# A fused linear attention and Fourier layer on one core: the channel transform on rows folded a second time, with parts of the weight and table conversion on POOL and a longer fixed order

## The chip, the core and the metric

The kernel runs on one core of a Trainium2 chip. The core has a matrix engine (PE, with its weight loads shown apart as PEld), two engines for elementwise work that also read the accumulators in PSUM (DVE and ACT), a third that works on SBUF alone (POOL), and SP, which issues most DMAs. PSUM has eight banks here, each 128 partitions by 512 fp32 values. The metric is the time of one execution on the device in microseconds; before the change its median is 1025.26 us over three runs.

## What is computed

Linear attention with an RMS norm, then a layer that adds the real part of a two-dimensional Fourier transform, then a normalised two-matrix network:

```python
def _attn_ref(q, k, v, g_norm):
    kv = np.einsum('bhsd,bhse->bhde', k, v)
    out = np.einsum('bhsd,bhde->bhse', q, kv)
    rms = np.sqrt(np.mean(out * out, axis=-1, keepdims=True) + 1e-06)
    return (out / rms * g_norm).astype(np.float32)

def _moe_ref(x, w_ch1, w_ch2):
    X = np.fft.fft(x, axis=1)
    X = np.fft.fft(X, axis=2)
    u = x + np.real(X).astype(np.float32)
    mu = np.mean(u, axis=-1, keepdims=True)
    var = np.mean((u - mu) ** 2, axis=-1, keepdims=True)
    un = (u - mu) / np.sqrt(var + 1e-06)
    ch = np.maximum(un @ w_ch1, 0.0) @ w_ch2
    return (u + ch).astype(np.float32)
```

There are 8 batches of 8 heads, 576 positions and head size 64; x is the attention's output with the heads side by side, 8 x 576 x 512. The network goes from 512 to 2048 and back. The two weight matrices arrive as 64-bit floats and are converted on the chip. A product in fp32 accuracy is made of three passes of the type fp32r: high by high, high by low, low by high part.

## The kernel before

The work has two parts. The first (to about 320 us) does attention and transforms for the eight batches, and with free time on PE the first piece of the network. The second is the rest of the network, and runs in the order in which it is written.

**The transforms.** The sequence axis is folded: a tile `x` of 96 or 97 rows holds position p and its mirror 576 - p side by side (512 columns each), three tiles a batch (`t` = 0, 1, 2). `plan_fold` scales the rows, adds to each channel d the mirror channel 512 - d (the tile `ab`, columns d = 1 to 256), and then takes sum and difference of the two sides (`xe`), which are split into high and low parts (`xh`, `xl`). Part 0 is the cosine part, part 1 the sine part. `plan_seq` transforms along the sequence: for each part and each half of the 256 channels (`ch`) nine matmuls of 290 columns into one bank (L816), then the high part by ACT (L830) and the low part by DVE (L834) into `pt`. `plan_chn` transforms along the channels: per tile and part six matmuls (two halves by three passes) of 258 columns (L851) with the table `cd`. ACT copies the cosine part (`me`, L863), DVE adds and subtracts the sine part (`pm`, L871), and the results are added to `x` on both sides (L883, L886; on POOL but for batch 0). Then `x` goes to memory (`u_scr`), is transposed by PE (L942) and split again (`unT`, L951 and L954). Channel 0 adds the same to every channel; it is summed apart (`zero`, L779), transformed once for all batches (L1131) and added as a bias at the end.

**Weights.** There are 16 blocks of each matrix. `plan_w` converts one: ACT takes the upper word's magnitude (L352), five DVE steps follow (a clamp, L359, then L360 to L369), a sum (L986), for the first matrix a mean taken off with PE's help (L383, L389), and a split into high and low parts. Blocks 0 to 2 are converted during the first batches, blocks 3 to 6 at the end of the first part, the rest in the second part by `sum_w` and `split_w`.

**Early network.** For each of nine blocks of 512 rows `plan_early` computes, with weight blocks 0 to 2, three times 12 matmuls of 512 columns (L424) and four times 9 (L442).

**Order.** The first part is a list of operations with engine, planned cost in ns, rank, predecessors and ring buffers. `Plan.run` simulates it: each engine takes the ready operation of the lowest rank whose buffers are free. Ranks come from batch and stage (`rank`), with shifts from the table `SHIFT`; FFN work has ranks from 1000, and 45 spare operations (two matmuls of 512 columns each on a constant, L494) have the last rank of all and keep PE running in gaps. Up to plan time `PIN_UNTIL` (in ns, 95000) the instructions of all engines are bound to this order; later ones may be moved by the scheduler of the language. `W_CONV` and `W_RANK` are the ranks at which weight blocks 0 to 2 are converted and loaded. Operations marked `port` are not planned beside one on POOL. PSUM banks are a ring of eight (`p8`).

Of the kernel before, what the change touches and what calls it, by code (L numbers as in the profile page):

```python
# [9 lines left out]
F32 = mybir.dt.float32  # L10
# [31 lines left out]
W_CONV = (-60, 5, 6)  # L42
W_RANK = (-60, 4, 11)
# [6 lines left out]
PIN_UNTIL = 95000  # L50
# [8 lines left out]
    ("", "POOL", 20): 18,  # L59
    ("chn", "ACT", -34): 54.5,  # L60
    ("dft", "DVE", -35): 83.5,
    ("fold", "DVE", -36): -33.5,
    ("out", "DVE", -58): 31,
    ("out", "ACT", 2): 157,
    ("q", "PE", -39): 3,
    ("q", "PE", 21): -30,
    ("q", "ACT", 31): -19.5,
    ("q_load", "DMA", -39): -1.5,
# [5 lines left out]
    "x": 8, "raw": 2, "e2": 4, "wk": 2, "xhl": 3, "pt": 1, "two": 2,   # L74
# [178 lines left out]
def kernel(  # L253
# [14 lines left out]
    nc = tc.nc  # L268
# [9 lines left out]
    ND = DH + 2  # L278
    W = DH + 1
# [71 lines left out]
    def w_clear(raw, ps):  # L351
        nc.scalar.activation(ps, w_raw(raw).bitcast(F32)[:, :, 1], AF.Abs)  # L352

    def w_steps(raw, ps, pf):
# [4 lines left out]
            lambda: nc.vector.tensor_scalar(ps, ps, F64_TINY, F64_HUGE, ALU.max, ALU.min),  # L359
            lambda: nc.vector.tensor_scalar(  # L360
                a, a, 3, 0x3FFFFFFF, ALU.logical_shift_left, ALU.bitwise_and
# [99 lines left out]
    cd = cst.tile([P, 2, 2, 2, ND], F32R, name="cd")  # L461
# [41 lines left out]
    def plan_dft(part, dst, src, n, r, key):  # L503
        size = src.shape[-2] * src.shape[-1]
# [5 lines left out]
        for lo_, hi_ in ((0, n - n % 16), (n - n % 16, n)):  # L510
# [8 lines left out]
            "DVE", 200 + 1.6 * size if key == "s" else 200 + size, r,  # L519
            lambda: nc.vector.tensor_tensor(lo, raw.t[:n, :size], hi.bitcast(F32), ALU.subtract),  # L520
            [b], [raw],
        )
        dft[key, part] = c

    last_qkv = []

    def plan_kv(b):
# [7 lines left out]
        for pr in range(NPAIR):  # L535
# [46 lines left out]
            mm.append(op("PE", 1080, rank(b, KV), go, ld + lds, [ps, kvt] + ts + rest))  # L582
# [48 lines left out]
    def plan_q(b, side, j, qt, ld):  # L631
# [17 lines left out]
        tr = op("PE", 330, rank(b, QT), turn, ld, [qt, ps, fq])  # L649
# [102 lines left out]
    def plan_fold(b, t, x, y_done, yp, gs):  # L752
# [25 lines left out]
        def zero():  # L778
            nc.scalar.activation(  # L779
                x0[:n, t, b : b + 1], xv(0)[:, 0:1], AF.Identity, bias=xv(1)[:, 0:1]  # L780
            )

        def fold():
            xx = x.t[:n].rearrange("p (s d) -> p s d", s=2)
            nc.vector.tensor_tensor(  # L785
                two_of(ab), xx[:, :, 1 : DH + 1], xx[:, ::-1, DM - 1 : DH - 1 : -1], ALU.add
            )
# [7 lines left out]
        f = op("DVE", 690, r, fold, ms, [x, ab, xe], port=True)  # L795
        z = op("ACT", 300, r, zero, ms + [i_x0], [x])
# [10 lines left out]
    def plan_seq(b, grp, xs, pt, dones):  # L807
        part, ch = divmod(grp, 2)
        ps = bank_buf("ps_f")

        def mm():
            idx = 0
            for t in range(3):
                n = rows[t]
                for a, c in passes:
                    nc.tensor.matmul(  # L816
                        ps.t[:, :NS],
                        xs[t].t[a][:n, part, ch * P : (ch + 1) * P],
                        cs[:n, part, c, t, :],
                        start=(idx == 0),  # L820
                        stop=(idx == 8),
                    )
                    idx += 1

        r = rank(b, SEQ)
        a = op("PE", 1200, r, mm, dones + [dft["s", part]], [ps, pt] + xs)
        a.dense = True
        h = op(
            "ACT", 414, r - D2,
            lambda: nc.scalar.activation(pt.t[0][:, part, ch, :], ps.t[:, :NS], AF.Copy), [a], [ps, pt],  # L830
        )

        def low():
            nc.vector.tensor_tensor(  # L834
                pt.t[1][:, part, ch, :], ps.t[:, :NS], pt.t[0][:, part, ch, :].bitcast(F32), ALU.subtract
            )

        return op("DVE", 450, r - D2, low, [h], [ps, pt])

    def plan_chn(b, t, x, pt, dones):  # L840
# [3 lines left out]
        for part in range(2):  # L844
            ps = bank_buf("ps_f")

            def mm(part=part, ps=ps):
                idx = 0
                for ch in range(2):
                    for a, c in passes:  # L850
                        nc.tensor.matmul(  # L851
                            ps.t[:n, :ND],
                            pt.t[a][:, part, ch, offs[t] : offs[t] + n],
                            cd[:, part, c, ch, :],
                            start=(idx == 0),
                            stop=(idx == 5),
                        )
                        idx += 1

            pss.append(ps)  # L860
            mms.append(op("PE", 720, r, mm, dones + [dft["d", part]], [ps, pt]))
        me, pm = e2_buf("me"), e2_buf("pm")
        c = op("ACT", 400, r - D2, lambda: nc.scalar.copy(me.t[:n, :W], pss[0].t[:n, :W]), mms[:1], [pss[0], me, pm])  # L863

        def pmv():
            return pm.t[:n, : 2 * W].rearrange("p (s w) -> p s w", s=2)

        pms = []
        for s in range(2):
            def mix(s=s):  # L870
                nc.vector.scalar_tensor_tensor(  # L871
                    pmv()[:, s], pss[1].t[:n, :W], sgn_t[:n, s, 0:1], me.t[:n, :W], ALU.mult, ALU.add
                )
# [43 lines left out]
    def plan_turn(b, side, t, x, done):  # L917
# [27 lines left out]
        a = op("PE", 330, r, turn, done, [x, ps] + blocks)  # L945
# [491 lines left out]
```

## Time and profile before

| | us |
|---|---|
| median of 3 runs | 1025.26 (1024.71 to 1025.57) |
| profiled execution | 1022.79 |
| its span | 1021.0 |
| PE busy, with overlaps of pipelined matmuls | 1002.3 |
| first matmul starts | 10.36 |
| last matmul of the channel transform starts (L851) | 318.8 |

The span is what the trace covers; the profiled execution's own time has 1.8 us around it. Lines L... are those of the kernel before. In the views below PE stands for matmuls, PEld for weight loads; a group's row gives its count, busy time and mean duration, then the idle time of the engine ahead of it. A matmul's duration covers its way through the array, so matmuls in a row overlap; how much time a group of them takes is read from the chain of work, whose pieces have a start and a length.

### The profile page before, as it was taken

What the parts mean: (1) busy time and instruction counts of PE and PEld (TensorE: products, weight loads), DVE (VectorE), ACT (ScalarE), POOL (GpSimd) and SP (SyncE); (2) the same over time, 40 slices, a digit from 0 to 9 for tenths busy, and PEclk for the clock granted to TensorE, in tenths of its full rate; (3) what the DMA queues carried; (4) which work ended last, traced back from release to release, by engine and by line L of the source; (5) the groups of instructions that cost most, each with busy time, mean ns of one, the idle gap of its engine ahead of it and who ended that gap; (6) DMA issues with size and microseconds to landing.
All of it is one profiled execution on the core that took longest, in us unless ns stands there. A gap on an engine that the chain in (4) does not pass through costs nothing.

```text
span 1021.0 us, 15425 instructions
## 1 busy us (share of the span) xinstructions
PE 1002.3 (98%) x6070; PEld 844.0 (83%) x6070; DVE 475.3 (47%) x847; ACT 324.8 (32%) x657; POOL 314.4 (31%) x328
## 2 busy tenths in 40 slices
PE   5999999999999999999999999999999999999997
PEld 5898888889888888888888888888888888888886
DVE  4897656654788879997131313131221311311211
ACT  2666556554644434344221202121121120210110
POOL 0526768775675132235722303020020010100000
PEclk9999999999999999999999999999999999999999
DMA  9989778664346775645553514230320400400101
GB/s 250 212 230 282 181 209 258 162 170 131 137 163 213 268 253 191 236 129 170 161 179 86 180 59 150 82 125 0 141 67 1 165 21 1 165 0 1 42 1 42
DMA packets 109260, 140.74 MB, mean 138 GB/s; under 512 B 51854, under 2 KB 76482, under 8 KB 104580
## 3 DMA queue, kind: packets, MB, share of 16 engines
q1 hardware_dynamic: 105652, 132.28, 41.9%
q0 software_dynamic: 1920, 6.29, 1.9%
q10 hardware_dynamic: 1616, 1.18, 0.5%
q8 instruction: 48, 0.79, 0.3%
q14 instruction: 24, 0.20, 0.1%
HBM read 88.33 MB, written 51.40 MB: 137 GB/s over the span
## 4 chain that ended last, share of the span: by engine, by line
PE 97%; DMA 1%; ACT 0%; POOL 0%; DVE 0%; issue 0%; SPq 0%; DVEq 0%; POOLq 0%
PE ps_h L424 38%; PE acc L442 38%; PE ps_o L669 4%; PE ps_f L816 4%; PE ps_f L851 4%; PE ps_k L574 3%; PE ps_s L494 2%; PE ps_q L643 2%; PE ps_t L942 2%; DMA qt<-in_q_dram 1%; PE ps_w L383 1%; DMA vm<-in_v_dram 0%; POOL x L883 0%; ACT x L686 0%; DVE uu L1324 0%
## 5 line engine op out<-in xcount | busy, mean ns | idle before, releaser
L424 PE MATMUL ps_h<-unTh,w 128*128 128x512 f32 x1152 | 356.6, 391 | 1.2 <-ACT fq L647 1.2
L442 PE MATMUL acc<-w,hh 128*128 128x512 f32 x1152 | 345.5, 390 | 0.0
L437 DVE SCALAR_TENSOR_TENSOR hl<-ps_h,hh 128x512 fp32r<-128x512 f32 x144 | 99.1, 688 | 371.8 <-ACT hh L434 367.5
L442 PEld LDWEIGHTS acc<-w,hh 128*128 128x128 f32 x1152 | 215.1, 188 | 44.3
L424 PEld LDWEIGHTS ps_h<-unTh,w 128*128 128x128 f32 x1152 | 214.8, 188 | 44.8 <-ACT fq L647 1.4
L434 ACT ACTIVATE hh<-ps_h 128x512 fp32r<-128x512 f32 x144 | 85.8, 596 | 454.0 <-PE ps_h L424 439.2
L424 PE MATMUL ps_h<-unTl,w 128*128 128x512 f32 x576 | 224.3, 389 | 0.0
L442 PE MATMUL acc<-w,hl 128*128 128x512 f32 x576 | 213.5, 389 | 0.0
L424 PEld LDWEIGHTS ps_h<-unTl,w 128*128 128x128 f32 x576 | 108.1, 188 | 22.6
L442 PEld LDWEIGHTS acc<-w,hl 128*128 128x128 f32 x576 | 108.1, 188 | 22.6
L1271 POOL DMA_INDIRECT uu<-u_scr,rowidx x24 | 23.2, 968 | 285.1 <-DVE uu L1324 177.9
L709 POOL TENSOR_TENSOR x<-x,gb 96x512 f32<-96x512 f32 (+1 forms) x42 | 55.0, 1330 | 45.7 <-ACT x L686 40.3
L1290 POOL TENSOR_TENSOR uu<-uu,up 128x512 f32<-128x512 f32 x36 | 45.7, 1298 | 45.2 <-ACT up L1287 45.2
L1234 POOL TENSOR_TENSOR w<-wap,w 128x512 fp32r<-128x512 f32 x18 | 26.4, 1467 | 75.3 <-ACT w L1233 69.1
L669 PEld LDWEIGHTS ps_o<-kvt,fq 64*96 64x96 f32 (+1 forms) x864 | 40.9, 162 | 5.7 <-issue 4.0
L1324 DVE SCALAR_TENSOR_TENSOR uu<-acc,rs_yb,uu 128x512 f32<-128x512 f32 x36 | 25.2, 744 | 42.5 <-PE acc L442 42.5
L669 PE MATMUL ps_o<-kvt,fq 64*96 64x64 f32 (+1 forms) x864 | 44.4, 248 | 0.0
L696 DVE TENSOR_REDUCE ss<-ps_o 96x8 f32<-96x512 f32 (+1 forms) x48 | 32.0, 682 | 26.5 <-ACT ps_o L691 26.3
L792 POOL TENSOR_TENSOR xe<-ab 96x256 f32<-96x256 f32 (+1 forms) x46 | 38.0, 845 | 18.7 <-DVE ab L785 17.9
L816 PE MATMUL ps_f<-cs,xh 96*128 96x290 f32 (+1 forms) x192 | 39.0, 300 | 0.0
L1278 DVE BATCH_NORM_STATS2 bst<-uu 128x6 f32<-128x512 f32 x36 | 24.5, 687 | 29.0 <-DMA uu<-u_scr,rowidx 19.8
L851 PE MATMUL ps_f<-cd,pt 128*96 128x258 f32 (+1 forms) x288 | 37.8, 285 | 0.0
(114 smaller groups left out, 1022.4 us busy)
## 6 DMA issues: line engine op xcount, KB each, us to landing
raw<-in_moe_w_ch_dram SPq DMA_DIRECT2D x32, 512.0 KB
unT_scr<-unTh SPq DMA_DIRECT2D x9, 1024.0 KB
unT_scr<-unTl SPq DMA_DIRECT2D x9, 1024.0 KB
part_scr<-part SPq DMA_DIRECT2D x36, 256.0 KB
unTh<-unT_scr SPq DMA_DIRECT2D x9, 1024.0 KB
unTl<-unT_scr SPq DMA_DIRECT2D x9, 1024.0 KB
up<-part_scr SPq DMA_DIRECT2D x36, 256.0 KB
out_dram<-uu SPq DMA_DIRECT2D x36, 256.0 KB
```

The lines of the kernel that those rows point to most:

```text
L424: nc.tensor.matmul(ps, w[c][:, kc * P : (kc + 1) * P], unT[a][:, kc, :], start=(idx == 0), stop=(idx == 3 * KC - 1),)
L434: nc.scalar.activation(hh, ps, AF.Relu)
L437: nc.vector.scalar_tensor_tensor(hl, ps, 0.0, hh.bitcast(F32), ALU.max, ALU.subtract)
L442: nc.tensor.matmul(acc, hpair[a][:, i * P : (i + 1) * P], w[c], start=(first and n == 0), stop=(last and n == 2),)
L574: nc.tensor.matmul(ps.t[s * D : (s + 1) * D, pr * D : (pr + 1) * D], km[:, s, j, :] if j < 4 else kr[:, h, :], vm[:, s, j, :] if j < 4 els ...
L669: nc.tensor.matmul(pss[s].t[:n, at : at + D], fqs[side].t[half, m, :n], kvt.t[half, m], start=True, stop=True,)
L696: nc.vector.tensor_reduce(ss.t[0][:n, :, t, s::2], pss[s].t[:n].rearrange("p (u m e) -> p u m e", u=2, e=D), AX.X, ALU.add,)
L709: nc.gpsimd.tensor_tensor(v_, v_, gb[:n].unsqueeze(1).to_broadcast([n, H, D]), ALU.mult)
L792: nc.gpsimd.tensor_tensor(o[:, s], a[:, 0], a[:, 1], ALU.subtract if s else ALU.add)
L816: nc.tensor.matmul(ps.t[:, :NS], xs[t].t[a][:n, part, ch * P : (ch + 1) * P], cs[:n, part, c, t, :], start=(idx == 0), stop=(idx == 8),)
L851: nc.tensor.matmul(ps.t[:n, :ND], pt.t[a][:, part, ch, offs[t] : offs[t] + n], cd[:, part, c, ch, :], start=(idx == 0), stop=(idx == 5),)
L1290: nc.gpsimd.tensor_tensor(us[j][i], us[j][i], part, ALU.add)
```

## The change

- **Second fold.** For cosine and sine, channel d and channel 256 - d differ only by a sign that depends on whether the output channel k is even or odd. `plan_fold` now writes the channels 129 to 255 in reverse, so that d and 256 - d stand in the same row of the two halves (three instructions in place of one). `plan_seq` handles both halves of a part together: the second bank is copied out by ACT (`far`), DVE forms sum and difference in the banks, and these, by the parity of k, are split into `pt`. In `plan_chn` each parity has its own three passes of 130 columns into its own half of the bank; the copies and sums after it read the two halves interleaved. The table `cd` holds even and odd columns of its first half alone, made by the new `plan_dft_d`. Channels 128 and 256 share a row: a factor `paired`, zero in that row, keeps them apart, and the part of channel 256 that is the same for all k is added to the sum of channel 0 (`zero`, now one DVE reduction).
- **POOL.** The low parts of the sequence table are made by POOL instead of DVE, and so is the clamp of weight blocks 0 to 2 (`w_clamp`; its input is in SBUF for these).
- **Order.** `PIN_UNTIL` goes from 95000 to 260000; `W_CONV` and `W_RANK` move weight blocks 1 and 2 later; `SHIFT` is another table; some planned costs differ (PE: `plan_kv` 1080 to 980, the transposes 330 to 378 and 360, `plan_seq` 1200 to 1250, `plan_chn` 720 to 570).

```diff
-W_CONV = (-60, 5, 6)
-W_RANK = (-60, 4, 11)
+W_CONV = (-60, 14, 16)
+W_RANK = (-60, 14, 21)
...
-PIN_UNTIL = 95000
+PIN_UNTIL = 260000
...
 SHIFT = {
...
+    ("fold", "POOL", 24): 102,
...
+    ("q", "PE", 41): 156.5,
...
-    "x": 8, "raw": 2, "e2": 4, "wk": 2, "xhl": 3, "pt": 1, "two": 2, 
+    "x": 8, "raw": 2, "e2": 4, "wk": 2, "xhl": 3, "pt": 1, "two": 2, "far": 1,
...
-    def w_clear(raw, ps):
-        nc.scalar.activation(ps, w_raw(raw).bitcast(F32)[:, :, 1], AF.Abs)
-
-    def w_steps(raw, ps, pf):
+    def w_clear(raw, to):
+        nc.scalar.activation(to, w_raw(raw).bitcast(F32)[:, :, 1], AF.Abs)
+
+    def w_clamp(eng, at):
+        eng.tensor_scalar(at, at, F64_TINY, F64_HUGE, ALU.max, ALU.min)
+
+    def w_steps(raw, ps, pf, high):
 
         a = ps.bitcast(U32)
         bits, low = w_raw(raw)[:, :, 1], w_raw(raw)[:, :, 0]
         return [
-            lambda: nc.vector.tensor_scalar(ps, ps, F64_TINY, F64_HUGE, ALU.max, ALU.min),
             lambda: nc.vector.tensor_scalar(
-                a, a, 3, 0x3FFFFFFF, ALU.logical_shift_left, ALU.bitwise_and
+                a, high.bitcast(U32), 3, 0x3FFFFFFF, ALU.logical_shift_left, ALU.bitwise_and
...
-    cd = cst.tile([P, 2, 2, 2, ND], F32R, name="cd")
+    cd = cst.tile([P, 2, 2, 2, NE], F32R, name="cd")
+
+    paired = cst.tile([P, 1], F32, name="paired")
+    nc.vector.tensor_scalar(paired, ident[:, P - 1 : P], -1.0, 1.0, ALU.mult, ALU.add)
...
     def plan_dft(part, dst, src, n, r, key):
+        if key == "d":
+            plan_dft_d(part, r)
+            return
...
-            "DVE", 200 + 1.6 * size if key == "s" else 200 + size, r,
-            lambda: nc.vector.tensor_tensor(lo, raw.t[:n, :size], hi.bitcast(F32), ALU.subtract),
+            "POOL", 2300, r,
+            lambda: nc.gpsimd.tensor_tensor(lo, raw.t[:n, :size], hi.bitcast(F32), ALU.subtract),
...
+    def plan_dft_d(part, r):
+        raw = ring("x", one, [P, 2 * DM], "draw")
+        pad = op("POOL", 100, r, lambda: nc.gpsimd.memset(raw.t[:, ND : 2 * NE], 0.0), kv_loaded, [raw])
+        c = dma(132, r, lambda: nc.sync.dma_start(raw.t[:, :ND], dft_d[part, :, 0]), kv_loaded, [raw])
+        def by_parity():
+            return raw.t[:, : 2 * NE].rearrange("p (k e) -> p e k", e=2)
+        if part == 0:
+            c = op(
+                "DVE", 200, r,
+                lambda: nc.vector.tensor_scalar(
+                    by_parity()[:, 1], by_parity()[:, 1], ident[:, P - 1 : P], None, ALU.add
+                ),
+                [c, pad], [raw],
+            )
+        hi, lo = cd[:, part, 0], cd[:, part, 1]
+        c = op("ACT", 360, r, lambda: nc.scalar.activation(hi, by_parity(), AF.Copy), [c, pad], [raw])
+        dft["d", part] = op(
+            "DVE", 420, r,
+            lambda: nc.vector.tensor_tensor(lo, by_parity(), hi.bitcast(F32), ALU.subtract), [c], [raw],
+        )
...
         def zero():
-            nc.scalar.activation(
-                x0[:n, t, b : b + 1], xv(0)[:, 0:1], AF.Identity, bias=xv(1)[:, 0:1]
-            )
+            nc.vector.tensor_reduce(x0[:n, t, b : b + 1], x.t[:n, :: DH], AX.X, ALU.add)
 
         def fold():
+
             xx = x.t[:n].rearrange("p (s d) -> p s d", s=2)
-            nc.vector.tensor_tensor(
-                two_of(ab), xx[:, :, 1 : DH + 1], xx[:, ::-1, DM - 1 : DH - 1 : -1], ALU.add
-            )
+            for at, lo, hi, step in ((0, 1, P + 1, 1), (P, DH - 1, P, -1), (DH - 1, DH, DH + 1, 1)):
+                width = (hi - lo) * step
+                nc.vector.tensor_tensor(
+                    two_of(ab)[:, :, at : at + width],
+                    xx[:, :, lo:hi:step],
+                    xx[:, ::-1, DM - lo : DM - hi : -step],
+                    ALU.add,
+                )
...
-        f = op("DVE", 690, r, fold, ms, [x, ab, xe], port=True)
-        z = op("ACT", 300, r, zero, ms + [i_x0], [x])
+        f = op("DVE", 860, r, fold, ms, [x, ab, xe], port=True)
+        z = op("DVE", 80, r, zero, ms + [i_x0], [x])
...
-    def plan_seq(b, grp, xs, pt, dones):
...
+    def plan_seq(b, part, xs, pt, dones):
+
+        pss, mms = [], []
         r = rank(b, SEQ)
-        a = op("PE", 1200, r, mm, dones + [dft["s", part]], [ps, pt] + xs)
-        a.dense = True
-        h = op(
-            "ACT", 414, r - D2,
-            lambda: nc.scalar.activation(pt.t[0][:, part, ch, :], ps.t[:, :NS], AF.Copy), [a], [ps, pt],
-        )
-
-        def low():
-            nc.vector.tensor_tensor(
-                pt.t[1][:, part, ch, :], ps.t[:, :NS], pt.t[0][:, part, ch, :].bitcast(F32), ALU.subtract
-            )
-
-        return op("DVE", 450, r - D2, low, [h], [ps, pt])
+        for ch in range(2):
+            ps = bank_buf("ps_f")
+
+            def mm(ch=ch, ps=ps):
+                idx = 0
+                for t in range(3):
+                    n = rows[t]
+                    for a, c in passes:
+                        nc.tensor.matmul(
+                            ps.t[:, :NS],
+                            xs[t].t[a][:n, part, ch * P : (ch + 1) * P],
+                            cs[:n, part, c, t, :],
+                            start=(idx == 0),
+                            stop=(idx == 8),
+                        )
+                        idx += 1
+
+            a = op("PE", 1250, r, mm, dones + [dft["s", part]], [ps, pt] + xs)
+            a.dense = True
+            pss.append(ps)
+            mms.append(a)
+        far = ring("far", one, [P, NS], "far")
+
+        def out_():
+            nc.scalar.copy(far.t, pss[1].t[:, :NS])
+
+        def add():
+            p0, p1 = (ps.t[:, :NS] for ps in pss)
+            if part == 0:
+                nc.vector.scalar_tensor_tensor(p1, far.t, paired, p0, ALU.mult, ALU.add)
+            else:
+                nc.vector.tensor_tensor(p1, p0, far.t, ALU.add)
+
+        def sub():
+            p0 = pss[0].t[:, :NS]
+            if part == 0:
+                nc.vector.scalar_tensor_tensor(p0, p0, paired, far.t, ALU.mult, ALU.subtract)
+            else:
+                nc.vector.tensor_tensor(p0, p0, far.t, ALU.subtract)
+
+        f = op("ACT", 410, r - D2, out_, mms[1:], [pss[1], far])
+        e = op("DVE", 450, r - D2, add, [mms[0], f], [far] + pss)
+        o = op("DVE", 450, r - D2, sub, [e], [far, pss[0]])
+        done = []
+        for ps, parity, after in ((pss[1], part, e), (pss[0], 1 - part, o)):
+            def high(ps=ps, parity=parity):
+                nc.scalar.activation(pt.t[0][:, part, parity, :], ps.t[:, :NS], AF.Copy)
+
+            def low(ps=ps, parity=parity):
+                nc.vector.tensor_tensor(
+                    pt.t[1][:, part, parity, :], ps.t[:, :NS],
+                    pt.t[0][:, part, parity, :].bitcast(F32), ALU.subtract,
+                )
+
+            h = op("ACT", 414, r - D2, high, [after], [ps, pt])
+            done.append(op("DVE", 450, r - D2, low, [h], [ps, pt]))
+        return done
...
-                idx = 0
-                for ch in range(2):
-                    for a, c in passes:
+                for e in range(2):
+                    for idx, (a, c) in enumerate(passes):
                         nc.tensor.matmul(
-                            ps.t[:n, :ND],
-                            pt.t[a][:, part, ch, offs[t] : offs[t] + n],
-                            cd[:, part, c, ch, :],
+                            ps.t[:n, e * NE : (e + 1) * NE],
+                            pt.t[a][:, part, e, offs[t] : offs[t] + n],
+                            cd[:, part, c, e, :],
                             start=(idx == 0),
-                            stop=(idx == 5),
+                            stop=(idx == 2),
                         )
-                        idx += 1
 
             pss.append(ps)
-            mms.append(op("PE", 720, r, mm, dones + [dft["d", part]], [ps, pt]))
+            mms.append(op("PE", 570, r, mm, dones + [dft["d", part]], [ps, pt]))
         me, pm = e2_buf("me"), e2_buf("pm")
-        c = op("ACT", 400, r - D2, lambda: nc.scalar.copy(me.t[:n, :W], pss[0].t[:n, :W]), mms[:1], [pss[0], me, pm])
+
+        def both(a):
+            return a[:n, : 2 * NE].rearrange("p (e k) -> p k e", e=2)[:, : ND // 2]
+
+        def single(a):
+            return a.rearrange("p (k e) -> p k e", e=2)
+
+        c = op(
+            "ACT", 400, r - D2,
+            lambda: nc.scalar.copy(single(me.t[:n, :ND]), both(pss[0].t)), mms[:1], [pss[0], me, pm],
+        )
 
         def pmv():
-            return pm.t[:n, : 2 * W].rearrange("p (s w) -> p s w", s=2)
+            return pm.t[:n, : 2 * ND].rearrange("p (s w) -> p s w", s=2)[:, :, :W]
 
         pms = []
         for s in range(2):
             def mix(s=s):
                 nc.vector.scalar_tensor_tensor(
-                    pmv()[:, s], pss[1].t[:n, :W], sgn_t[:n, s, 0:1], me.t[:n, :W], ALU.mult, ALU.add
+                    single(pm.t[:n, s * ND : (s + 1) * ND]), both(pss[1].t), sgn_t[:n, s, 0:1],
+                    single(me.t[:n, :ND]), ALU.mult, ALU.add,
                 )
 
...
         a = dma(512, r if r_load is None else r_load, lambda: w_load(which, f, raw.t), after, [raw])
         src = ring("wk", one, [P, DM], "wa") if which == 1 else ps
-        d = op("ACT", 670, r, lambda: w_clear(raw.t, ps.t), [a], [raw, ps, pf, src])
+
         late_ = f >= NA
-        for n, cost in enumerate((690, 690, 690, 680, 760)):
+        high = ps if late_ else pf
+        d = op("ACT", 670, r, lambda: w_clear(raw.t, high.t), [a], [raw, ps, pf, src])
+        if late_:
+            d = op("DVE", 690, r, lambda: w_clamp(nc.vector, ps.t), [d], [ps])
+        else:
+            d = op("POOL", 1000, r, lambda: w_clamp(nc.gpsimd, pf.t), [d], [pf])
+        for n, cost in enumerate((690, 690, 680, 760)):
             d = op(
-                "DVE", cost, r, lambda n=n: w_steps(raw.t, ps.t, pf.t)[n](), [d], [raw, ps, pf],
-                port=(n == 4),
+                "DVE", cost, r, lambda n=n: w_steps(raw.t, ps.t, pf.t, high.t)[n](), [d],
+                [raw, ps, pf], port=(n == 3),
...
-        pts = [plan_seq(b, grp, xhl, pt, lows) for grp in range(4)]
+        pts = sum((plan_seq(b, part, xhl, pt, lows) for part in range(2)), [])
```

More of the change, by code (lines that the diff above doesn't have):

```diff
@@ L58 @@
 SHIFT = {
[L59 to L68, printed above, removed]
+    ("dft_d", "ACT", -35): -14,
+    ("fold", "DVE", 14): -1.5,
+    ("fold", "ACT", 24): 55,
+    ("fold", "POOL", 24): 102,
+    ("kv", "DMA", 10): 1.5,
+    ("out", "ACT", 12): 31,
+    ("out", "DVE", 12): -81,
+    ("out", "PE", 12): 2,
+    ("out", "PE", 22): 87.5,
+    ("q", "ACT", 31): -12,
+    ("q", "PE", 41): 156.5,
+    ("seq", "ACT", 35): -40,
+    ("turn", "DVE", -33): 11,
+    ("w", "DVE", 16): -60.5,
+    ("y", "DVE", -37): 73.5,
+    ("y", "DVE", 13): -35.5,
+    ("y", "POOL", 23): -4.5,
 }
@@ L278 @@
     ND = DH + 2
+    NE = DH // 2 + 2
     W = DH + 1
@@ L580, in go @@
                         )
-            mm.append(op("PE", 1080, rank(b, KV), go, ld + lds, [ps, kvt] + ts + rest))
+            mm.append(op("PE", 980, rank(b, KV), go, ld + lds, [ps, kvt] + ts + rest))
         done = op(
@@ L647, in take @@
             nc.scalar.copy(dst[:, :, TR - 1 :: -1] if side else dst, view())
-        tr = op("PE", 330, rank(b, QT), turn, ld, [qt, ps, fq])
+        tr = op("PE", 378, rank(b, QT), turn, ld, [qt, ps, fq])
         done.append(op("ACT", 490, rank(b, QT), take, [tr], [ps, fq]))
@@ L805, in plan_fold @@
         return xhl, op("POOL", 1340, r, low, [h], [xe, xhl]), z
-    def plan_seq(b, grp, xs, pt, dones):
-        part, ch = divmod(grp, 2)
-        ps = bank_buf("ps_f")
-        def mm():
-            idx = 0
-            for t in range(3):
-                n = rows[t]
-                for a, c in passes:
[L816 to L821, printed above, removed]
-                    )
-                    idx += 1
-        r = rank(b, SEQ)
-        a = op("PE", 1200, r, mm, dones + [dft["s", part]], [ps, pt] + xs)
-        a.dense = True
-        h = op(
-            "ACT", 414, r - D2,
-            lambda: nc.scalar.activation(pt.t[0][:, part, ch, :], ps.t[:, :NS], AF.Copy), [a], [ps, pt],
-        )
-        def low():
-            nc.vector.tensor_tensor(
-                pt.t[1][:, part, ch, :], ps.t[:, :NS], pt.t[0][:, part, ch, :].bitcast(F32), ALU.subtract
-            )
-        return op("DVE", 450, r - D2, low, [h], [ps, pt])
+    def plan_seq(b, part, xs, pt, dones):
+        pss, mms = [], []
+        r = rank(b, SEQ)
+        for ch in range(2):
[47 more added lines that the diff above has]
+        return done
@@ L944, in plan_turn @@
         r = rank(b, NRM)
-        a = op("PE", 330, r, turn, done, [x, ps] + blocks)
+        a = op("PE", 360, r, turn, done, [x, ps] + blocks)
         for j, lo, hi, at, step in pieces:
@@ L1217, in sum_w @@
         w_clear(raw, ps)
-        for step in w_steps(raw, ps, pf):
+        w_clamp(nc.vector, ps)
+        for step in w_steps(raw, ps, pf, ps):
             step()
```

3 lines of the change are left out of this document (removed).

## The prediction, made before the result

> **What bounds the kernel now.** I read the engine totals and the chain that ended last, then the stretches of time, then the waits of PE.
>
> ```profile
> span 1021.0 us, 15425 instructions
> PE 1002.3 (98%) x6070; PEld 844.0 (83%) x6070; DVE 475.3 (47%) x847; ACT 324.8 (32%) x657; POOL 314.4 (31%) x328
> ...
> PEclk9999999999999999999999999999999999999999
> ...
> PE 97%; DMA 1%; ACT 0%; POOL 0%; DVE 0%; issue 0%; SPq 0%; DVEq 0%; POOLq 0%
> ```
>
> ```profile
> 12.00:95.00 83.00, 83.00 (x970) 70.77 (x971) 65.78 (x112) 44.91 (x99) 28.31 (x41) 1.00 0.97 247
> 95.00:260.00 165.00, 162.01 (x1590) 142.03 (x1586) 92.69 (x175) 92.42 (x216) 117.07 (x129) 1.00 0.69 192
> 260.00:330.00 70.00, 70.00 (x463) 61.35 (x462) 57.47 (x103) 37.98 (x85) 46.65 (x48) 1.00 0.46 161
> ```
>
> ```profile
> PE ps_q L643 <- DMA qt<-in_q_dram: 10.4, 1, 10.4
> PE ps_h L424 <- ACT fq L647: 1.2, 1, 1.2
> PE ps_k L574 <- DMA vm<-in_v_dram: 1.0, 1, 1.0
> PE ps_t L942 <- POOL x L883: 0.4, 1, 0.4
> ```
>
> The columns of the stretches are length, then busy time of PE, PEld, DVE, ACT and POOL, granted clock, DMA share and GB/s. The chain is PE for 97% of the span, at full clock. After the first load PE waits some 3 us in all (165.00 - 162.01). So the time is the sum of what PE issues; another engine counts only where it makes PE wait. One part of that sum is filler:
>
> ```profile
> L494 PE MATMUL ps_s<-still x90: 387/397/588, 13.4 to 90.4; 128*128 128x512 f32 x90
> ```
>
> The 45 spare operations (90 matmuls, all between 13.4 and 90.4 us) keep PE running where the plan has nothing for it. The change keeps their number, so they cost the same afterwards, and what PE does not need inside the first 90 us buys nothing by itself.
>
> **The channel transform.** What PE issues changes in one place: the 288 matmuls of L851 stream 130 columns instead of 258. Their number, their weights (96 or 97 columns) and their passes stay.
>
> ```profile
> L851 PEld LDWEIGHTS ps_f<-cd,pt x288: 159/162/167, 61.4 to 318.7; 128*96 128x96 f32 x93, 128*97 128x97 f32 x51
> L851 PE MATMUL ps_f<-cd,pt x288: 276/282/362, 61.4 to 318.8; 128*96 128x258 f32 x93, 128*97 128x258 f32 x51
> ```
>
> ```profile
> 32.49 2.87 PE ps_o L669 x64
> ```
>
> ```profile
> 307.33 4.84 PE ps_f L816 x36
> 312.17 0.18 PE ps_t L1163
> 312.35 0.42 PE ps_w L383 x2
> 312.76 2.07 PE acc L442 x9
> 314.83 4.30 PE ps_f L851 x36
> 319.13 6.13 PE acc L442 x27
> 325.26 2.73 PE ps_h L424 x12
> 327.99 0.22 PE ps_w L383 x2
> ```
>
> These are pieces of the chain (start, length, what). A batch's 36 matmuls take 4.30 us, 119.4 ns each; a 512-column matmul takes 2.73/12 = 227 ns. The line through these two has a slope of 0.424 ns a column, which puts 130 columns at **65 ns**, if streaming sets the pace. The upper end is L383, ordinary fp32 with 128 columns: 0.22 us for two issues, **110 ns**.
>
> Between them stands the weight load, because every matmul has one:
>
> ```profile
> L494 PEld LDWEIGHTS ps_s<-still x90: 186/188/337, 13.3 to 90.2; 128*128 128x128 f32 x90
> L669 PEld LDWEIGHTS ps_o<-kvt,fq x864: 156/162/163, 24.1 to 283.0; 64*96 64x96 f32 x116, 64*97 64x97 f32 x57
> L1131 PEld LDWEIGHTS ps_o<-cs,x0h x6: 87/89/91, 301.0 to 302.0; 96*8 96x8 f32 x4, 97*8 97x8 f32 x2
> ```
>
> A load's duration grows from 89 ns at 8 columns to 188 at 128, 0.825 ns a column, so 96 columns occupy the load path for about 79 ns, more than the 65 ns of streaming. L669 is the row that shows this limit at work: weights of the same 96 columns, only 64 moving columns. Its matmuls go in pairs, each on its own half of the rows, and 32 pairs take 2.87 us, 90 ns a pair. I take **90 ns**, this row, because it has the same load and less to stream. The gain is 288 x (119.4 - 90) = **8.5 us**; by the ends it is 15.7 us (65 ns) and 2.7 us (110 ns).
>
> The Trainium skill, "TensorE: Matmul & The Clock Gate", section "Back-to-back issue gap", says that load and matmul together set the sustained spacing, about 81 ns at 128 columns and 131 at 512. By its figure the gain would be an estimated 288 x (119.4 - 81) = 11.1 us. The trace differs at 512 columns (227 ns), so I leave the sum at the measured row.
>
> **What is added beside PE.** The second fold costs, per batch, two ACT copies and four DVE operations on 290 columns, plus two more fold instructions per tile.
>
> ```profile
> L834 DVE TENSOR_TENSOR pt<-ps_f,pt 128x290 fp32r<-128x290 f32 x32 | 13.8, 454 | 9.4 <-ACT pt L830 9.2
> L830 ACT ACTIVATE pt<-ps_f 128x290 fp32r<-128x290 f32 x32 | 12.9, 415 | 15.0 <-PE ps_f L816 14.7
> L785 DVE TENSOR_TENSOR ab<-x x23: 673/717/1861, 32.5 to 299.5; 96x512 f32<-96x512 f32 x15, 97x512 f32<-97x512 f32 x8
> L1282 DVE TENSOR_SCALAR bm<-bmv 128x4 f32<-128x4 f32 x9 | 1.5, 166 | 0.2
> L779 ACT ACTIVATE x<-x x24: 278/294/301, 36.3 to 294.7; 96x1 f32<-96x1 f32 x16, 97x1 f32<-97x1 f32 x8
> L359 DVE TENSOR_SCALAR ps_a<-ps_a x32: 674/698/702, 6.6 to 473.4; 128x512 f32<-128x512 f32 x32
> L520 DVE TENSOR_TENSOR cs<-draw,cs x2: 996/1022/1048, 33.3 to 34.2; 97x870 fp32r<-97x870 f32 x2
> L1290 POOL TENSOR_TENSOR uu<-uu,up 128x512 f32<-128x512 f32 x36 | 45.7, 1298 | 45.2 <-ACT up L1287 45.2
> ```
>
> DVE gains 32 x 0.454 = 14.5 us for the sums and differences. The fold's extra instructions are bounded by nothing and by two of 0.166 us on each of 24 tiles, 8 us; I take 5. The first column's sum moves from ACT (24 x 0.294 = 7.1 us) to DVE (24 x 0.166 = 4.0). DVE loses six clamps (4.2 us) and the low parts of the sequence table (2.0). Net it is about +17 us before 330 us, where DVE is now busy for 65.78 + 92.69 + 57.47 = 216 of 318 us: 73% instead of 68%. ACT gets 16 x 0.415 = 6.6 us and loses 7.1. POOL gets six clamps, each between nothing and L1290's 1.3 us, 8 us at most, and two low parts, planned at 2.3 us each. In 12 to 95 us POOL is busy 28 of 83, so it has room. None of the three becomes the bound, and I cost all this at **nothing**, covered by PE's own work.
>
> What can break that cover is latency. From the end of L816 to the start of L851 the change puts a copy (0.415), a sum and a difference (0.454 each) ahead of the old copy and subtraction: about 1.3 us more, in which two PSUM banks per part stay taken. The ring "far" has one buffer, so the second part's copy waits on ACT until the first part's difference is done, with the high copies queued behind it and PE behind those. In batch 7 above, 312.17 to 314.83 is 2.66 us of other work; L442 pieces stand right behind it to lengthen it. If nothing filled it, eight batches would lose 8 x 1.3 = 10 us. The strided reads of the two halves in PSUM carry the same element count as L863 and L871 now; I cost them at nothing, with half their duration more as the other end, off PE's path.
>
> **The order.** The conversions of weight blocks 1 and 2, and their four loads of 512 KB, move behind most of batch 1's work in the plan. At 247 GB/s a load is 2.1 us on SP's queue, so 8.5 us of transfers step aside for q, k and v of batches 1 and 2, and four conversions of seven or eight DVE steps of about 0.69 us leave the time of batch 0. Against that stands the first block's FFN work, which comes later (second rival). The order is fixed to 260 us of plan time instead of 95. It covers the stretch with the 3 us of waits, and can remove them or add its own: minus 3 to plus 10 us (the unfilled latency above). I take zero. The shifts of ranks and planned durations cost nothing themselves; they act through the order.
>
> **The sum** for the profiled execution: 1022.79 us (span 1021.0 and 1.8 around it) - 8.5 = 1014.3. The median of the runs is 1025.26, so the forecast is 1025.26 - 8.5 = **1016.8 us**.
>
> **The rivals.**
>
> 1. *Streaming alone sets the pace* (65 ns): L669's pace could come from its fp32 data or its pairing instead of its load. Against it, the 79 ns slope. Gain 15.7: 1009.6 us.
>
> 2. *The first blocks come too late; slower.* The spares are used up at 90 us, and these pieces stand about there:
>
> ```profile
> 77.36 5.48 PE ps_h L424 x24
> ...
> 84.60 2.97 PE ps_h L424 x12
> ...
> 89.88 0.96 PE ps_s L494 x4
> 90.84 2.06 PE acc L442 x9
> ```
>
> A block's early FFN is 36 + 36 such matmuls, 72 x 0.227 = 16.3 us. Two thirds of its first half and all of its second need weight blocks 1 and 2. If these come late and the work of batches 1 and 2 does not come forward in their place, PE idles with no filler left. All of it uncovered gives 1016.8 + 16.3 = 1033 us, and it is slower than before from 8.5 us on, half of it. For it: DMA is at 0.97 in this stretch, so batch 2 can hardly arrive much earlier. Against it: DVE is relieved just there, and PE had 20 us of filler to displace. The same skill page ("HAM oscillation") has PE's clock halve after a pause of more than about 3.4 us. The longest wait here after the start is 1.2 us, at clock 1.00, so no run here shows it.
>
> 3. *Narrow matmuls run like ordinary fp32*, as two issues: L383's 0.22 us a product instead of 119.4 ns. All fp32r matmuls of this trace have 258 columns or more, so nothing excludes it. 288 x 0.10 = 29 us more: 1054 us.
>
> 4. *Half the gain is eaten*: 110 ns a matmul (1022.6), or waits of PE of 4 to 10 us from the fixed order or the longer way from L816 to L851 (1021 to 1027). Here the change does what it says, and the time hardly shows it.
>
> **How the numbers follow.** Forecast 60%, own range 1013 to 1020.5 (waits of -3 to +4 us); rival 1 10%; rival 4 15%, of which 8 below, 5 within and 2 above the bound of 0.2% (2.05 us, about what a measurement of this kernel can tell from no change); rival 2 10%, nearly all slower, 1 within; rival 3 5%. Faster: 60 + 10 + 8 = 78%; within: 5 + 1 = 6%; slower: 2 + 9 + 5 = 16%. The range runs from rival 1 to the middle of rival 4, 1009 to 1024, and leaves out rivals 2 and 3 and the ends, some 20%.
>
> **What would show it.** Right: L851's successor at about 3.2 us for 36 in the chain, 130-column forms, load durations still 162 ns, PE's total about 8.5 us less, waits of PE after 12 us at 3 us or less. The stretch 12 to 95 with PE at 83 of 83 speaks against rival 2; a wait of PE on a DVE weight conversion or on a q, k or v load between 80 and 110 us for it. A piece of 36 at 2.4 us is rival 1, at 4.0 us or above rivals 3 and 4. The forecast is wrong if PE waits on the new sums (DVE) or on PSUM banks, or if the spares are no longer all inside the gaps.

## The result, and the profile after

The changed kernel takes **1018.55 us** (median of 4 runs, 1018.16 to 1020.03) against 1025.41 for the kernel before beside it: a ratio of 0.9932, 95% interval 0.9915 to 0.995. The gain is 6.9 us; forecast were 8.5 and 1016.8 us. The profiled execution took 1020.03 us, the slowest of the four.

The page's totals, then the stretches of time (length, busy PE, PEld, DVE, ACT, POOL, granted clock, DMA share, GB/s) and PE's waits, all of the kernel after, with its own line numbers (L830 is the fold, L849 POOL's low part `xl`, L908 the low part of `pt`, L867 and L927 the two transforms):

```profile
span 1018.2 us, 15524 instructions
PE 995.1 (98%) x6070; PEld 836.4 (82%) x6070; DVE 497.2 (49%) x945; ACT 326.4 (32%) x649; POOL 323.6 (32%) x338
...
PE 87%; DVE 7%; issue 2%; DMA 1%; POOL 1%; ACT 1%; SPq 0%; DVEq 0%; POOLq 0%; ACTq 0%
```

```profile
12.00:95.00 83.00, 82.08 (x998) 69.57 (x1000) 60.98 (x115) 45.14 (x97) 41.23 (x53) 1.00 0.85 216
95.00:260.00 165.00, 163.53 (x1642) 144.47 (x1638) 128.05 (x263) 101.96 (x227) 120.41 (x132) 0.99 0.76 213
260.00:330.00 70.00, 67.42 (x419) 58.31 (x418) 57.14 (x115) 32.40 (x75) 41.08 (x44) 0.95 0.42 148
```

```profile
PE ps_w L393 <- DVE wa L1078: 11.8, 1, 11.8
PE ps_f L927 <- DVE pt L908: 2.0, 1, 2.0
PE ps_o L713 <- DVE ss L740: 0.8, 2, 0.6
PE ps_f L867 <- POOL xl L849: 0.8, 1, 0.8
...
```

The chain is no longer PE almost alone: DVE has 7% of it. Between 95 and 260 us PE gets more done than before (1642 matmuls against 1590), but it starts later, and between 260 and 330 us the clock is down to 0.95. The channel transform itself did what was forecast, as its line and one piece of the chain show (L927 is the old L851):

```profile
L927 PEld LDWEIGHTS ps_f<-cd,pt x288: 159/165/289, 65.4 to 315.5; 128*96 128x96 f32 x96, 128*97 128x97 f32 x48
L927 PE MATMUL ps_f<-cd,pt x288: 223/248/425, 65.4 to 315.6; 128*96 128x130 f32 x96, 128*97 128x130 f32 x48
```

```profile
215.56 3.04 PE ps_f L927 x36
234.32 4.86 PE ps_f L867 x36
245.63 3.05 PE ps_f L927 x36
```

36 matmuls take 3.04 us, 84 ns each; forecast were 90.

Two places give time back. **The start:** PE's first matmul now waits for the first weight conversion, and in that one stands POOL's clamp, 1.92 us where DVE took 0.69:

```profile
L363 DVE TENSOR_SCALAR ps_a<-ps_a x26: 680/692/711, 271.0 to 474.6; 128x512 f32<-128x512 f32 x26
L363 POOL TENSOR_SCALAR wp<-wp x6: 1916/1917/1931, 6.1 to 108.4; 128x512 f32<-128x512 f32 x6
```

PE starts at 11.76 us instead of 10.36. **The pause at 288 us**, in the timeline of POOL, DVE and PE (start, length; idle time before it in brackets):

```profile
286.41 2.86 POOL L849 TENSOR_TENSOR xl<-xe,xh 97x512 fp32r<-97x512 f32 x2
```

```profile
285.69 3.60 DVE L830 TENSOR_TENSOR ab<-x 96x256 f32<-96x256 f32 x3
289.22 0.17 DVE L1216 TENSOR_TENSOR x0l<-x,x0h 97x24 fp32r<-97x24 f32 x1
289.31 0.81 DVE L908 TENSOR_TENSOR pt<-ps_f,pt 128x290 fp32r<-128x290 f32 x2
```

```profile
289.81 2.57 PE L927 MATMUL ps_f<-cd,pt 128*96 128x130 f32 x14 [1.95 <-DVE pt L908]
```

Three fold instructions of DVE take 3.60 us beside two subtractions of POOL; over the whole kernel the median of this line is 0.42 us, from 0.15 to 1.53. The Trainium skill, "SBUF — State Buffer", section "SBUF: two separate sides", says that DVE, for an operation with two inputs in SBUF, and GpSimd hold a shared port exclusively, and the loser blocks; these rows agree. The low part that the channel transform needs stands behind the fold on DVE, and PE waits 1.95 us for it. Then its clock is halved, as the stretches cut at that point show:

```profile
102.51:290.25 187.74, 184.93 (x1780) 163.06 (x1779) 150.18 (x310) 113.24 (x252) 135.14 (x150) 1.00 0.67 198
290.25:297.08 6.83, 6.83 (x30) 5.40 (x29) 3.46 (x10) 1.27 (x3) 5.49 (x6) 0.52 0.10 27
297.08:1017.00 719.92, 714.39 (x3225) 592.09 (x3223) 273.48 (x494) 160.24 (x285) 132.71 (x116) 1.00 0.33 112
```

The 0.99 between 95 and 260 us is a shorter spell of the same kind, 3.41 us long, behind a wait of only 0.82 us:

```profile
98.41 0.40 PE L867 MATMUL ps_f<-cs,xl 96*128 96x290 f32 x1 [0.82 <-POOL xl L849]
```

```profile
99.10:102.51 3.41, 3.41 (x17) 3.41 (x17) 2.36 (x5) 0.48 (x2) 3.24 (x6) 0.55 1.24 217
```

So the balance seemed plain: near 10 us from the stream, 1.4 lost at the start, and 1.95 and about half of 6.83 at the pause. But that leaves some 3 us, and 6.9 were measured. The experiments show that it is not the balance.

### The profile page after: what moved, and what is told of

Its sections match the earlier page's. It is cut to its first block, busy times and chain, and to the rows that moved or that the text cites. A ratio compares the mean times of both kernels' runs of the same rounds, so it can differ in the third digit from the quotient of the medians.

```text
span 1018.2 us, 15524 instructions
## 1 busy us (share of the span) xinstructions
PE 995.1 (98%) x6070; PEld 836.4 (82%) x6070; DVE 497.2 (49%) x945; ACT 326.4 (32%) x649; POOL 323.6 (32%) x338
## 4 chain that ended last, share of the span: by engine, by line
PE 87%; DVE 7%; issue 2%; DMA 1%; POOL 1%; ACT 1%; SPq 0%; DVEq 0%; POOLq 0%; ACTq 0%
PE ps_h L434 36%; PE acc L452 35%; PE ps_f L867 3%; PE ps_o L713 3%; PE ps_k L618 3%; PE ps_f L927 2%; PE ps_s L507 2%; PE ps_q L687 1%; PE ps_t L1028 1%; DVE ab L830 1%; DMA part_scr<-part 1%; DVE wp L379 1%; PE ps_w L393 1%; DVE unTl L1040 1%; DVE ss L740 1%
## 5 line engine op out<-in xcount | busy, mean ns | idle before, releaser
L1327 POOL TENSOR_TENSOR w<-wap,w 128x512 fp32r<-128x512 f32 x18 | 23.3, 1294 | 71.3 <-ACT w L1326 71.3
L867 PE MATMUL ps_f<-cs,xh 96*128 96x290 f32 (+1 forms) x192 | 41.1, 308 | 0.1
L830 DVE TENSOR_TENSOR ab<-x 96x254 f32<-96x254 f32 (+5 forms) x69 | 39.2, 622 | 0.1
```

Source lines behind the costliest of these rows:

```text
L830: nc.vector.tensor_tensor(two_of(ab)[:, :, at : at + width], xx[:, :, lo:hi:step], xx[:, ::-1, DM - lo : DM - hi : -step], ALU.add,)
L867: nc.tensor.matmul(ps.t[:, :NS], xs[t].t[a][:n, part, ch * P : (ch + 1) * P], cs[:n, part, c, t, :], start=(idx == 0), stop=(idx == 8),)
```

## The experiments

The theory at first was that of the prediction: the gain is PE's shorter stream, less these two places. The rival was that the gain comes from the order. Kernels sent together ran on one chip, in four groups: 1 to 4, 5 to 8, 9 to 11, and 12. A difference between groups is one between chips as well; the medians of the kernel before differ by 0.7 us among the groups (1024.59 to 1025.32). Here are the medians; "ratio" is to the kernel before on the same chip, with its interval.

| | kernel | us (lowest to highest) | ratio |
|---|---|---|---|
| 1 | after, stream at 260 columns | 1024.71 (1023.50 to 1026.09) | 0.9999 [0.9986, 1.0012] |
| 2 | after, two of three passes at 66 columns | 1022.04 (1017.59 to 1023.39) | 0.9966 [0.9948, 0.9985] |
| 3 | after, order fixed to 95 us | 1035.91 (1034.31 to 1040.60) | 1.0121 [1.0087, 1.0154] |
| 4 | after, order fixed to 330 us | 1017.13 (1016.02 to 1019.97) | 0.9928 [0.9901, 0.9954] |
| 5 | after, again | 1019.05 (1018.57 to 1019.93) | 0.9947 [0.9929, 0.9965] |
| 6 | before, narrow stream | 1024.73 (1021.38 to 1034.06) | 1.0015 [0.9983, 1.0047] |
| 7 | before, order fixed to 260 us | 1016.64 (1016.27 to 1016.90) | 0.9923 [0.9906, 0.9940] |
| 8 | after, clamp on DVE | 1015.30 (1015.07 to 1018.18) | 0.9919 [0.9897, 0.9941] |
| 9 | before, 6 and 7 together | 1016.22 (1016.07 to 1016.71) | 0.9908 [0.9882, 0.9934] |
| 10 | after, 4 and 8 together | 1013.63 (1013.39 to 1014.48) | 0.9883 [0.9857, 0.9909] |
| 11 | after, ranks and shifts of before | 1028.11 (1023.50 to 1031.04) | 1.0017 [0.9996, 1.0037] |
| 12 | before, order fixed to 330 us | 1019.22 (1018.81 to 1020.38) | 0.9942 [0.9919, 0.9964] |

### 1. The stream made wide again

```diff
-                            ps.t[:n, e * NE : (e + 1) * NE],
+                            ps.t[:n, : 2 * NE],
...
-                            cd[:, part, c, e, :],
-                            start=(idx == 0),
-                            stop=(idx == 2),
+                            cd[:, part, c].rearrange("p e k -> p (e k)"),
+                            start=(e == 0 and idx == 0),
+                            stop=(e == 1 and idx == 2),
```

> The changed kernel with the order and the loads kept, but each channel matmul streams both halves of the table (260 columns; this spoils the result of the channel transform). Theory 1, the gain is the shorter stream of L927, 288 matmuls at 86 ns instead of 119: the width gives 288 x 0.034 = 9.8 us back, 1028 us. Rival, most of the gain came from the longer fixed order and the moved work: under 3 us of it go, 1019 to 1021 us.

1024.71 us: 5.7 to 6.2 more than the changed kernel (1019.05 and 1018.55). A batch's matmuls are back at 119 to 120 ns each, so PE issues nearly 10 us more, but the time rises by some 6. The clock of the profiled execution is back at 0.999, without a spell of half clock; that of run 5 has one of 6.83 us, by which it loses an estimated 3.4 us, half of it. In this kernel's own order the narrow stream is thus worth about six tenths of what it saves on PE, and part of the rest is lost by the clock: the theory holds in direction, not in size.

### 2. An even narrower stream

```diff
+                        to = NE if idx == 0 else 66
...
-                            ps.t[:n, e * NE : (e + 1) * NE],
+                            ps.t[:n, e * NE : e * NE + to],
...
-                            cd[:, part, c, e, :],
+                            cd[:, part, c, e, :to],
```

> The changed kernel with two of three passes of the channel transform cut to 66 columns (the low parts of the other columns are left out). Theory 1, the weight load of 96 columns sets 86 ns a matmul: no change, 1018.5 plus or minus 1 us, and 36 matmuls still take 3.1 us. Rival, streaming sets the pace: 192 x 0.027 = 5.2 us less, 1013 us.

The chain of this kernel (the matmuls are on L928 here):

```profile
161.01 3.01 PE ps_f L928 x36
178.02 3.19 PE ps_f L928 x36
218.45 3.02 PE ps_f L928 x36
```

Half the columns in two of three passes leave a batch's 36 matmuls at 3.01 to 3.19 us: streaming does not set the pace. That leaves the weight load, which no run changed. The time, 1022.04, is not the unchanged one that was expected. Its runs are spread over 6 us, and its profile shows a spell of halved clock at another place (0.98 between 12 and 95 us). The granted clock is 0.992 to 0.994 in eight of its ten runs and 0.996 in three of the changed kernel's four, an estimated 2 to 4 us of 1020. Why this kernel pauses there was not followed further.

### 3, 4, 7 and 12. How far the order is fixed

Only the constant differs: 95000 and 330000 in the changed kernel, 260000 and 330000 in the kernel before.

```diff
-PIN_UNTIL = 260000
+PIN_UNTIL = 95000
```

> The changed kernel with the order fixed to 95 us of plan time only, as before. Theory 1, the order is worth little by itself, and the pause of PE at 288 us with the halved clock behind it is an accident of where DVE's fold meets POOL: the pause goes or moves, 1014 to 1020 us. Rival, the longer fixed order carries part of the gain: 1022 us or more, with PE's waits between 95 and 260 us back at 3 us or above.

1035.91 us: 17 us slower than the changed kernel. The rival held, and more than held. The first theory had put the order at nothing. Part of the 17 us is the clock: 0.989 to 0.990 is granted where the changed kernel has 0.994 to 0.996, an estimated 4 to 7 us of 1036.

> The changed kernel with the order fixed to 330 us of plan time. Theory 1, the pause at 288 us comes from operations behind the fixed stretch, where DVE's fold runs beside POOL: with the plan's order there it goes, clock 1.00, 4 to 5 us less, 1014 us. Rival, the pause is in the plan's order itself or a longer fixed order makes new waits: 1018 us or more.

1017.13 us, the pause behind the fold gone from PE's waits. That is 1.4 to 1.9 less than the changed kernel, not 4 to 5: the clock stays at 0.995, with other spells of half speed. The runs of the two kernels overlap (1016.02 to 1019.97 here, 1018.16 to 1020.03 there), so even this gain is not sure.

> The kernel before with the order fixed to 260 us of plan time, nothing else changed. If fixing the order is a gain by itself (it took 17 us to undo it in the changed kernel), 1022 us or less, with PE's waits of 3 us between 95 and 260 us gone. If it only fits the order that it was made for, 1024 us or more.

**1016.64 us, from the constant alone**, without the second fold, the POOL parts or the new ranks: 8.7 us less than the kernel before and 2.4 less than the changed kernel on the same chip. The stretches and PE's waits between 95 and 335 us of this kernel:

```profile
95.00:260.00 165.00, 162.71 (x1658) 143.94 (x1655) 96.04 (x185) 99.58 (x229) 122.56 (x135) 1.00 0.72 201
260.00:330.00 70.00, 70.00 (x452) 61.58 (x451) 56.38 (x104) 36.09 (x83) 42.42 (x44) 1.00 0.45 157
```

```profile
PE ps_o L669 <- ACT fq L647: 1.3, 1, 1.3
PE acc L442 <- DVE ss L696: 0.6, 1, 0.6
PE ps_q L643 <- DVE ss L696: 0.2, 1, 0.2
```

The PE column hardly moves (162.71 against 162.01), but in the same 165 us there are 1658 matmuls instead of 1590. What goes are delays too short for the busy time, which overlaps, or the waits to show. Counting each matmul of the stretch at the distance that its kind keeps in an undisturbed row (227 ns for 512 columns, 133.5 for 290, 119.5 for 258, 82 for the transposes, 45 and 41 for the two 64-column kinds), the work is 147.8 us before and 154.7 here. The kernel before lost 17 us of the 165, and only 3.2 of that were pauses of more than 0.35 us; with the order fixed 10 us are lost. Shown is that the constant alone gives the gain; that it comes from these short delays is read from the count.

> The kernel before with the order fixed to 330 us of plan time, nothing else changed (to 260 us: 1016.6). Theory 2, nearly all of the change's gain is the fixed order: 1015 to 1017 us, at or below the changed kernel's 1018.6 to 1019.1. Rival, only the stretch to 260 us matters or a longer one brings waits of PE: 1018 us or more.

1019.22 us: the rival. 70 us more of fixed order cost some 2.6 us in the old kernel (on another chip than run 7) and gain 1.4 to 1.9 in the new one, or 1.7 with the clamp on DVE (run 10 beside 8, also on two chips). These are small differences; they suggest that how far the order should be fixed belongs to each kernel, and it was found by trying.

### 5. The changed kernel again

> The changed kernel itself, as the yardstick on this chip: 1018 to 1020 us, one pause of PE of about 2 us near 288 us and a granted clock of about 0.996.

1019.05 us, clock 0.995, the same pause. This is the yardstick for 6 to 8.

### 6 and 9. The narrow stream in the old kernel

```diff
-                            ps.t[:n, :ND],
+                            ps.t[:n, : ND if idx == 0 else 130],
...
-                            cd[:, part, c, ch, :],
+                            cd[:, part, c, ch, : ND if idx == 0 else 130],
```

> The kernel before with five of the six channel matmuls of a part cut from 258 to 130 columns (the rest of the columns keep only the first pass), nothing else changed; behind 95 us of plan time the scheduler may order anew. Theory 1, the shorter stream alone is worth 240 x 0.033 = 8 us: 1017 us. Rival, in the old order PE arrives early at the same operands and waits: the gain shrinks below 3 us, 1022 us or more, with new waits or a clock below 1.00.

1024.73 us: nothing gained, the rival. The runs spread from 1021.4 to 1034.1, and the profiled one has its clock at 0.93 between 95 and 260 us. The scheduler also ordered this kernel anew behind 95 us, so order and stream are not apart here; that is what run 9 does.

> The kernel before with both the order fixed to 260 us and the channel matmuls cut as in the experiment with the narrow stream alone (five of six passes at 130 columns, the other columns keep one pass). Fixed order alone gave 1016.6 us, the narrow stream alone 1024.7. Theory 2, in a fixed order PE's shorter work counts in full: 240 x 0.033 = 8 us less, 1009 us. Rival, the first part cannot feed PE faster in any order, and what PE saves turns into waits and a halved clock: 1014 us or more.

**1016.22 us, where 1009 were expected**: 0.4 less than with the fixed order alone (on another chip; by the ratios it is 1.5, within their intervals), though the distances behind the channel matmuls fall from 35.0 to 27.3 us, and the clock is 0.999 in both. PE's waits between 95 and 335 us, beside those of run 7 above:

```profile
PE ps_o L669 <- ACT fq L647: 3.1, 2, 1.8
PE ps_f L816 <- POOL xl L801: 1.8, 2, 1.1
PE ps_o L1131 <- DVE x0h L1123: 0.8, 1, 0.8
PE ps_h L424 <- DVE ss L696: 0.6, 1, 0.6
PE ps_w L383 <- POOL wp L379: 0.6, 1, 0.6
PE ps_o L1131 <- DVE x0l L1124: 0.5, 1, 0.5
PE ps_q L643 <- DVE ss L696: 0.4, 1, 0.4
PE acc L442 <- DVE ss L696: 0.4, 1, 0.4
```

Their sum is 8.2 us against 2.1. Most of the 8 us saved on PE come back as waits, spread over ACT, POOL and DVE: in this order the first part seems to run at the pace at which the batches get through the other engines, while PE looks 96% busy (159.17 of 165 us between 95 and 260). This disproves, for the old order, the prediction's step from PE's work to the time.

### 8 and 10. The clamp back on DVE

```diff
-            d = op("POOL", 1000, r, lambda: w_clamp(nc.gpsimd, pf.t), [d], [pf])
+            d = op("POOL", 1000, r, lambda: w_clamp(nc.vector, pf.t), [d], [pf])
```

> The changed kernel with the clamp of weight blocks 0 to 2 back on DVE at the same place of the order. POOL's clamp takes 1.93 us in the profile after, DVE's 0.70, and PE's first instruction waits for it: theory 1, PE starts 1.2 us earlier, at 10.5 us, and the time falls by 0 to 1.2 us. Rival, six more operations on DVE delay the transform chain of batch 0: the same time or slower by up to 4 us.

1015.30 us, 3.7 less than the changed kernel on the same chip, and three times the most that was expected. In SBUF DVE's clamp takes 0.43 us, as the timeline of this kernel shows beside the start of PE:

```profile
6.21 0.43 DVE L363 TENSOR_SCALAR wp<-wp 128x512 f32<-128x512 f32 x1 [4.14 <-ACT wp L360]
...
10.32 2.08 PE L393 MATMUL ps_w<-wa,mean_t 128*128 128x128 f32 x8 [10.32 <-DVE wa L1078]
```

1.5 us of the gain are this start. The pause at 288 us is still there (1.95 us), but only 3.41 us of half clock follow in place of 6.83:

```profile
288.45:291.86 3.41, 3.41 (x18) 2.52 (x17) 1.86 (x6) 0.90 (x2) 2.42 (x4) 0.50 0.02 5
```

How the rest of the gain divides was not separated.

> The changed kernel with the clamp back on DVE (1015.3 us alone) and the order fixed to 330 us of plan time (1017.1 us alone, where the changed kernel has 1018.6 to 1019.1). If the two mend different places (PE's start and the pause at 288 us): 1013 to 1014 us. If both only shift the same pause: 1015 us or more.

**1013.63 us**, 11.6 less than before (ratio 0.9883): the best version of the study, better than both kernels and than run 7. Within the spread of the runs the two add up; the start is at 10.27 us and no wait of PE behind it is longer than 1 us.

### 11. The new operations with the old ranks

`SHIFT`, `W_CONV`, `W_RANK` and the planned PE costs of the kernel before but for the channel transform's, everything else as changed.

```diff
-W_CONV = (-60, 14, 16)
-W_RANK = (-60, 14, 21)
+W_CONV = (-60, 5, 6)
+W_RANK = (-60, 4, 11)
...
-            a = op("PE", 1250, r, mm, dones + [dft["s", part]], [ps, pt] + xs)
+            a = op("PE", 1200, r, mm, dones + [dft["s", part]], [ps, pt] + xs)
```

> The changed kernel's operations (second fold, POOL parts, order fixed to 260 us) with the ranks, shifts and PE costs of the kernel before. Theory 2, the second fold is worth its PE time and the new ranks are not needed: 1008 to 1013 us. Rival, the second fold nets nothing beside the fixed order, because DVE and the longer way to the channel transform cost what PE saves: 1016 us or more, with waits of PE on the new sums or on POOL's clamp.

1028.11 us: slower than the changed kernel by 9 us, though the order is fixed to 260 us here too. Its runs spread over 7.5 us. The profiled one, 1029.67 us, has a wait of 1.95 us for POOL's `xl` in the sequence transform (L860 here), and less than 1 us behind it the clock falls:

```profile
126.97 0.40 PE L860 MATMUL ps_f<-cs,xl 96*128 96x290 f32 x1 [1.95 <-POOL xl L842]
```

```profile
95.00:127.82 32.82, 29.75 (x336) 25.87 (x336) 27.30 (x55) 18.96 (x40) 26.62 (x32) 1.00 0.68 183
127.82:151.71 23.89, 23.50 (x161) 21.38 (x162) 11.68 (x27) 9.27 (x24) 10.84 (x14) 0.50 0.52 142
151.71:260.00 108.29, 106.97 (x1054) 93.95 (x1052) 75.94 (x161) 64.54 (x145) 73.50 (x79) 1.00 0.66 197
```

PE is busy for 23.50 of 23.89 us, at half clock. With the old ranks, shifts and planned costs together, which were not taken apart, PE arrives too early at low parts (0.52 us for `pt` and 1.95 us for `xl` in the 7 us ahead of this stretch), pauses, and then pays with its clock.

## Why the prediction was right, and where it was not

The time fell inside the range and the sign was right, 1.8 us from the forecast. Its steps fared unequally.

- **"90 ns, this row."** Right, and as far as tested for its reason. Matmuls of 130 columns stand 84 to 86 ns apart; half the columns left that unchanged (run 2), which rules out streaming and leaves the load. PE's term was 288 x 0.033 to 0.035, 9.5 to 10 us, not 8.5. Rivals 1 and 3 are out.
- **"So the time is the sum of what PE issues."** This is the step that failed. The narrow stream is worth 5.7 to 6.2 us in the new order (run 1), where half clock takes back part of it, and 0.4 in the old one with the order fixed (run 9 beside 7). A chain that is 97% PE did not mean that PE set the pace: the chain goes from matmul to matmul even where each stands a little apart from the last.
- **"The order ... I take zero"**, between -3 and +10 us. Too narrow at the lower end and wrong in value: by itself it is worth -8.7 us in the kernel before (run 7), and undone in the changed kernel +17 (run 3). The "3 us of waits" in the stretch were a fifth of what PE lost there.
- **POOL's clamp "between nothing and L1290's 1.3 us".** It takes 1.92 us, above the upper end, and it stood on the path of PE's first matmul, where I had costed it at nothing: 3.7 us in all, 1.5 of them at the start (run 8).
- **DVE's load, "about +17 us before 330 us"**: it rose by 29.0 us there (221.2 to 250.2), and by 21.9 in total. The term that was too small is the fold, taken at 5 us more: its line went from 23.6 to 40.0 us. Covered as a load, but not as an order: the fold beside POOL made the pause at 288 us. The prediction had named DVE's new sums and a lack of banks as what might make PE wait; it was the fold in front of the low part.
- **Rival 2**, the first blocks too late, did not come: PE is busy for 82.08 of 83.00 us between 12 and 95 us. **Rival 4**, a part of the gain eaten by waits, is what happened to the stream. PE's waits behind the start sum to 5.8 us, where the prediction had named 3 or less as the sign of being right. That the time still came out near the forecast is due to the order, which the sum did not have; to that extent it is luck.

The parts do not add: order, ranks and stream depend on each other, as runs 3, 7, 9 and 11 show, so the 6.9 us cannot be shared out among them. What the second fold brings beside the best order for the old operations stays open; runs 7 and 12 are only two orders of many.

## What to carry to other kernels

A chain that is nearly all PE and few waits do not show that PE sets the pace: count the matmuls in a stretch at their undisturbed distance, and what is missing is the most that a better order can give there (17 us in the kernel before, of which fixing the order gave back 7). Make the shorter operation alone, in a fixed order, before counting its time as a gain. And when work moves to an engine with time to spare, look whether the moved step stands on a path that PE waits for, and take its duration from a row of the same kind on that engine.

## What the hardware showed that was not expected

- **PE's clock halves after short pauses, and stays down while PE is busy.** Waits of 1.95 us were enough (the kernel after at 288 us; run 11, with further waits of 0.4 to 0.6 us near it), and in three profiles one of 0.81 or 0.82 us (the kernel after at 98 us, runs 8 and 10 at 97 us). The spells last 3.41 us or multiples of it: 6.83 us at 288 us, 23.89 us in run 11. The length of one wait does not decide it: the same wait of 0.82 us in runs 1, 4 and 5, of which run 5 is the same kernel, was followed by no spell. Nor was any wait between the first load and the end in the kernel before and in runs 7 and 9, where the longest was 1.8 us. What does decide stays open here. The Trainium skill, "TensorE: Matmul & The Clock Gate", section "HAM oscillation", puts the limit at pauses of more than about 3.4 us; the runs here show half clock after shorter ones.
- **The clamp, an operation with one input, is slow on POOL:** 1.92 us for 128 x 512 in SBUF, against 0.43 on DVE in SBUF and 0.69 on DVE in PSUM. The subtraction of two inputs of almost the same size takes POOL 1.29 us (L849).
